# Seven products instead of eight in two groups of an expert layer, one bank copy more, and kept sums weighed in three steps

## The chip, the cores and the metric

The kernel runs on one core of one Trainium2 chip. The core has a matrix engine (TensorE, PE in the profile; PEld is its loading of weights), VectorE (DVE), ScalarE (ACT), GpSimd (POOL) and SyncE (SP, which here only issues transfers). The metric is the device time of one execution in microseconds; before the change the median of 4 runs is 928.86 us (928.18 to 929.29).

## The reference

A polynomial-sketch attention is followed by a mixture of eight experts whose weights come from eight rounds of Sinkhorn normalisation. All is fp32.

```python
# attention: B, H, S, D = 4, 4, 1088, 32; r = 8
phi(x) = outer product of (S1 x) and (S2 x), flattened      # 64 features
kv, z  = phi(k)^T v, sum over s of phi(k)
x      = (phi(q) kv) / (phi(q) z + 1e-6)    # laid out as N = 4352 rows of 128
# routing
P = exp(x @ w_gate - max)
8 times: P /= P.sum(1) + 1e-9;  P /= P.sum(0) + 1e-9;  P *= N / 8
# experts: F = 1024
out = sum over e of P[:, e] * (relu(x @ w1[e]) @ w2[e])
```

## The kernel before, in words

The experts are nearly all of the work, and the kernel starts them long before the routing weights exist. x is kept transposed (xT, 128 features by 4352 rows). The work is cut into **groups** (L647 to L656): a range of rows, cut into two or three tiles of n columns, and a list of experts.

- Groups 0 to 7 are **unweighted**: expert 0 on all 4352 rows, and expert 1 on rows 0 to 1280, computed without the routing weight, while attention and routing still run. Their results stay in SBUF as *kept sums* (kept[0], kept[1]) and are weighed later. Group 0 is rows 0 to 512 with n = 256 and expert 0, group 1 rows 512 to 1088 with n = 288 and expert 0, group 2 rows 0 to 512 with n = 256 and expert 1; groups 3 to 5 have n = 416, groups 6 and 7 n = 384.
- Groups 8 to 13 are **weighted**: x is multiplied by the expert's routing weight beforehand (POOL, L693, tile xe), so that the sums over the remaining experts add up in PSUM. Five of them have three tiles of 256 (twenty products for a block, from ten sums of pieces of w2, tile ws4, made by POOL at L242 for the first weighted group and stored in DRAM for the others), the last has two.

A group and an expert make an item, and an item is cut into blocks. A block has **steps**; each step is a first-layer product (x by w1, L929, two halves of 64 output columns side by side) with its relu by ScalarE (L933, tile hb or hx), and, eight steps late (LAG), the second-layer products of an earlier block (L1114, function into). These are half-width products too, two of which run beside each other. They add up in PSUM banks s0 to s3, and part(g, k) is called when bank k of a group has its last product.

For two tiles, the second layer is done in one of two ways:

- **eight** (L1017): the plain way, eight products for a block, no other work. part copies the two banks to kept (ScalarE, L736). Used by groups in DIRECT.
- **seven**: a Strassen-Winograd scheme (L1026). VectorE makes three subtractions for a block, one of double width (function less, L946, called at steps 4 and 5 after the block begins), the weights need four sums of w2 (tile ws, made by POOL at L203 to L206 in sums_of_two), and the seven sums of products, p1 to p7, lie in four banks. part_of_seven then recombines them: ScalarE copies halves of banks to tiles z, m, w, f and r (L762 to L777), and VectorE adds (L756 for those that are to go soon, in the next step, L753 for those at leisure). P1 lies in the lower half of bank 0, and L769 adds it, from the bank, to the copy m of bank 1.

What sets the order: DVE and PE run in the order of the program until some way into the last unweighted group, and the scheduler orders the other engines, except that instructions under keep_in_program_order keep theirs (POOL's weighings and their transfers among them). steps() is a generator that yields each step's share of time (n/480, and 16/15 of that for a group in DIRECT); fill(n) runs steps until n units are used up. The attention of batches 1 to 3 (function attention) and the routing (function routing) yield how many units of expert work are to go between their own pieces.

In attention(b), keys_sums is PE's L352 (it needs the key products, kp, L336), times(b, c) is VectorE's L468 and needs the tile rb from a transfer, keys_kept copies a key sum to kvs (VectorE L368), tops is PE's L477 with the bank from L472, over is VectorE's reading of that bank (L490 to L496), and keys_ab(b + 1) is PE's L319. The query transfers to qa and qb are issued in part by POOL.

weigh_kept (L709) weighs the kept sums of a weighted group's rows on POOL, each with a transfer of weights from pT to the tile pb, and adds them; steps() calls it in one of the group's experts. last_part writes the last group's two halves, y1 and y2.

Of the kernel before, what the change touches and what calls it, by code (L numbers as in the profile page):

```python
# [50 lines left out]
def kernel(  # L51
# [12 lines left out]
    nc = tc.nc  # L64
# [50 lines left out]
    own = consts.tile([P, H], F32, name="own")  # L115
# [36 lines left out]
    for i in range(2):  # L152
        t = wk.tile([P, H + 1, NT + 1, D], F32, name=f"v{i}", bufs=1)
# [487 lines left out]
    lower, upper = slice(0, H2), slice(H2, P)  # L641
# [8 lines left out]
    PLAIN = len(groups)  # L650


    DIRECT = (0, 1, 2)
    for lo in (1280, 512, 2048, 2816, 3584):
        groups.append((lo, NT3, 3, list(range(2 if lo == 512 else 1, E)), True))
    groups.append((0, 256, 2, list(range(2, E)), True))  # L656
# [2 lines left out]
    kept = [keep.tile([P, N], F32, name="kept0"), keep.tile([P, 1280], F32, name="kept1")]  # L659
# [4 lines left out]
    def direct_of(j):  # L664
        return items[j][0] in DIRECT

# [20 lines left out]
    def weights_of(e, lo, n, tag):  # L687
        pb = pools[0].tile([P, 3 * NT3], F32, tag=tag, name=tag)[:, 0:n]
        tc.keep_in_program_order(nc.sync.dma_start(out=pb, in_=pT[e:e + 1, lo:lo + n].to_broadcast([P, n])))
        return pb  # L690

    def weigh(out, x, pb):
        tc.keep_in_program_order(nc.gpsimd.tensor_tensor(out, x, pb, op=Alu.mult))  # L693
# [12 lines left out]

    first_weighted = next(j for j, (g, e) in enumerate(items) if g == PLAIN)

    def weigh_kept(g):  # L709

        lo, n, t, es, _ = groups[g]
        ys = []
        for e in range(es[0]):
            ys.append(kept[e][:, lo:lo + n * t])
            weigh(ys[e], ys[e], weights_of(e, lo, n * t, "pb"))
        for y in ys[1:]:
            tc.keep_in_program_order(nc.gpsimd.tensor_tensor(ys[0], ys[0], y, op=Alu.add))
        if t == 2:
            k1, k2 = ys[0][upper, 0:n], ys[0][upper, n:2 * n]
            tc.keep_in_program_order(nc.gpsimd.tensor_tensor(k1, k1, k2, op=Alu.subtract))  # L720
# [5 lines left out]
    def put(y, lo, n, queues):  # L726
        b0, nb = lo // 32, n // 32
        yt = pools[0].tile([P, NT3 // 32, 32], F32, tag="yt", name="yt", bufs=4)[:, 0:nb, :]
        nc.vector.transpose(out=yt.rearrange("p b d -> p (b d)"), in_=y)
        store(yt, b0, b0 + nb, queues)  # L730

    def part(g, k):

        if g in DIRECT:
            lo, n, _, es, _ = groups[g]
# [8 lines left out]
    def room(tag, n=NMAX):  # L744
        return keep.tile([P, NMAX], F32, tag=tag, name=tag)[:, 0:n]

    def part_of_seven(g, k):

        lo, n, _, es, _ = groups[g]
        s = sums[g][k]  # L750

        def add(out, a, b):
            at_leisure(lambda: nc.vector.tensor_tensor(out, a, b, op=Alu.add))  # L753

        def add_now(out, a, b):
            soon.append(lambda: nc.vector.tensor_tensor(out, a, b, op=Alu.add))  # L756

        own = parts.setdefault(g, {})
        y1, y2 = (kept[es[0]][:, lo + t * n:lo + (t + 1) * n] for t in range(2))
        if k == 0:  # L760
            z = own["z"] = room("z", n)
            nc.scalar.copy(z[lower], s[upper])  # L762
            nc.scalar.copy(z[upper], s[lower])
            add_now(z, s, z)
            own["p1"] = s
        elif k == 1:
            m = own["m"] = room("m", n)
            nc.scalar.copy(m, s)
            add_now(y1[lower], own["p1"][lower], m[lower])  # L769
        elif k == 2:  # L770
            w, f = own["w"], own["f"] = room("w", n), room("f", n)
            nc.scalar.copy(w[lower], s[lower])
            nc.scalar.copy(f[lower], s[upper])
            nc.scalar.copy(f[upper], s[upper])
        else:
            r = room("r", n)
            nc.scalar.copy(r[upper], s[lower])  # L777
            own["r"] = r
            own["p7"] = s
        own[k] = True  # L780
        z, w, f, m = (own.get(x) for x in "zwfm")
        if all(own.get(x) for x in (0, 2, 3)) and "v" not in own:
            own["v"] = True
            add_now(w[upper], own["p7"][upper], own["r"][upper])
            add(z, z, w)
            add(y2, z, f)
        if all(own.get(x) for x in range(4)):
            add(y1[upper], z[upper], m[upper])
# [9 lines left out]
    def last_part(g, k):  # L798


        lo, n, *_ = groups[g]
        s0, s1, s2, s3 = sums[g]

        def add(out, a, b):
            nc.vector.tensor_tensor(out, a, b, op=Alu.add)

        (y1, y2), z, w, x, f, r = last_rooms(g)
        if k == 3:
            nc.scalar.copy(r[upper], s3[lower])
            add(w[upper], s3[upper], r[upper])  # L810
        elif k == 0:
            nc.scalar.copy(z[upper], s0[lower])
            nc.scalar.copy(f, s0)
            add(x[upper], z[upper], w[upper])
            add(z[upper], x[upper], s0[upper])
        elif k == 2:
            nc.scalar.copy(r[lower], s2[upper])
            nc.scalar.copy(x[lower], s0[lower])
            add(y2[upper], z[upper], s2[upper])
            add(y2[lower], s2[lower], r[lower])  # L820
            put(y2, lo + n, n, (nc.sync, nc.scalar))
            add(x[upper], x[upper], s2[upper])
        else:
            add(y1, s1, x)
            put(y1, lo, n, (nc.sync, nc.scalar))
# [298 lines left out]
    def steps():  # L1124

        todo, sums_at, t = {}, {}, 0
        for k in range(len(blocks) + 5):
            if k == len(blocks) - 2:
                ctx.enter_context(tc.manual_schedule(engines={engines.DVE, engines.PE, engines.Activation}))
            if k == len(blocks):  # L1130
                for i, ps in enumerate(last_products()):
                    todo.setdefault(t + i, []).extend(ps)
            if k < len(blocks):
                j, q = blocks[k]
                g, e = items[j]
                lo, n, tiles, es, weighted = groups[g]
                if q == 0:
                    for i in (j, j + 1, j + 2 if 0 < j and j + 2 < first_weighted else j):
                        if i < len(items) and i not in sources and (pools or i < first_weighted):
                            prepare_x(i)  # L1140
                        if i < len(items) and i not in loaded_w and (pools or i < first_weighted):
                            prepare_w(i)
                if j == 0 and q == 2:
                    prepare_w(2)
                if q == 1 and j + 1 < first_weighted and not direct_of(j + 1) and loaded_w[j + 1][2] is None:
                    w1, w2, _ = loaded_w[j + 1]
                    w = w1, w2, sums_of_two(items[j + 1][1], w2)
                    loaded_w.update({i: w for i in loaded_w if items[i][1] == items[j + 1][1]})
                if q == 0:
                    if weighted and e == es[3 if tiles == 3 else 2]:  # L1150
                        weigh_kept(g)
                if k == len(blocks) - HELD:
                    kept_to_sums(g)
                m, step, sums_ = (four if tiles == 3 else two)(k)
                products = twenty if tiles == 3 else eight if g in DIRECT else seven
            for c in range(m if k < len(blocks) else 4):
                if k < len(blocks):
                    step(c)
                for do in sums_at.pop(t, ()):
                    do()  # L1160
                while soon:
                    soon.pop(0)()
                for b, p in todo.pop(t, ()):
                    second(b, p)
                if k < len(blocks) and c == 0:
                    for i in range(2, 10):
                        sums_at.setdefault(t + i, []).append(lambda i=i, f=sums_: f(i))
                    if k < len(blocks) - 2:
                        for i, ps in enumerate(products(k)):
                            todo.setdefault(t + LAG + i, []).extend((k, p) for p in ps)  # L1170
                share = n / 480 * (16 / 15 if g in DIRECT else 1)
                if k >= len(blocks):
                    while later:
                        later.pop(0)()
                elif later and (tiles == 3 or c % 2 or share > 0.9):
                    later.pop(0)()
                yield share
                t += 1
        while soon:
            soon.pop(0)()  # L1180
        while later:
            later.pop(0)()
# [105 lines left out]
```

## Time and profile before

| what | us |
|---|---|
| median of 4 runs | 928.86 |
| the profiled execution | 929.29 |
| its span in the trace | 927.5 |
| PE busy in the span | 913.6 |
| DVE, ACT, POOL busy | 675.8, 411.9, 210.9 |
| unweighted group 0: first product L929 | 16.9 |
| bank copies of group 2 (L736) end | 93.2 |
| routing's transfer to pT issued | 174.57 |
| first weighted product (L929 on xe) | 191.66 |
| last matmul ends | 920.8 |

Times on the trace count from the start of the span; the execution's own time is 1.8 us more than the span. An engine's row gives the start, the length, the engine, the line, the operation and its tiles (output<-inputs, partitions x elements), how many instructions are merged (x), and in brackets how long the engine had been idle before it and what released it. A matmul of fp32 is two instructions of PE, so the x of such a row counts twice.

### The profile page before, as it was taken

The page shows a single profiled execution, that of the slowest core. Times are in us where ns is not written, and L with a number is a line of the kernel's source. Part 1 is how long each engine was busy: PE and PEld are TensorE (multiplying, and loading weights), DVE is VectorE, ACT ScalarE, POOL GpSimd, SP SyncE. Part 2 cuts the span into 40 slices and gives each one's busy share as a digit, 9 for nine tenths or more (in the row PEclk, how much of TensorE's full clock was granted, in tenths as well). Part 3 has the DMA queues.
Part 4 walks back from the last instruction along what each step waited for, and adds up shares of the span by engine and source line. Part 5 has one row for each costly group of instructions (what it writes and reads, how often), then busy time and mean ns, then how long its engine had stood idle before and what let it go on. Part 6 is the DMA issues. An engine that isn't in the chain of part 4 may idle for free.

```text
span 927.5 us, 18876 instructions
## 1 busy us (share of the span) xinstructions
PE 913.6 (98%) x7466; PEld 544.9 (59%) x7466; DVE 675.8 (73%) x1140; ACT 411.9 (44%) x888; POOL 210.9 (23%) x220
## 2 busy tenths in 40 slices
PE   9999999999999999999999999999999999999997
PEld 6777444456666666655555555555555555556865
DVE  8544688797779797785976566966667977768665
ACT  3333455553444454434544444544445444446443
POOL 4021300093546402030120101101110234221120
PEclk9999999999999999999999999999999999999999
DMA  9994100213454445453445433363434366443640
GB/s 260 303 275 151 52 1 1 84 49 109 133 157 160 153 136 139 139 180 109 148 126 161 141 127 130 114 188 125 149 108 163 100 193 206 159 170 92 179 147 12
DMA packets 91303, 128.13 MB, mean 138 GB/s; under 512 B 25392, under 2 KB 69504, under 8 KB 86480
## 3 DMA queue, kind: packets, MB, share of 16 engines
q1 hardware_dynamic: 88384, 121.42, 42.1%
q0 software_dynamic: 1600, 5.36, 1.9%
q8 instruction: 58, 0.95, 0.4%
q10 hardware_dynamic: 1232, 0.16, 0.1%
q14 instruction: 29, 0.24, 0.1%
HBM read 107.88 MB, written 19.05 MB: 137 GB/s over the span
## 4 chain that ended last, share of the span: by engine, by line
PE 94%; DVE 4%; issue 1%; ACT 1%; DMA 0%; DVEq 0%; ACTq 0%
PE a L929 49%; PE s L1114 41%; PE a L352 1%; PE a L477 1%; DVE hb L993 1%; DVE hx L946 0%; PE a L319 0%; DVE pqg L993 0%; PE s L384 0%; PE a L441 0%; DMA raw<-in_S_dram 0%; ACT hb L933 0%; PE s L407 0%; DVE kept L756 0%; PE a L511 0%
## 5 line engine op out<-in xcount | busy, mean ns | idle before, releaser
L929 PE MATMUL a<-xe,w 128*64 128x256 f32 (+1 forms) x2560 | 517.3, 470 | 0.0
L933 ACT ACTIVATE hb<-a 128x256 f32<-128x256 f32 (+4 forms) x408 | 195.0, 479 | 258.5 <-PE a L929 230.6
L933 ACT ACTIVATE hx<-a 128x256 f32<-128x256 f32 (+1 forms) x360 | 167.2, 465 | 215.1 <-PE a L929 195.3
L929 PEld LDWEIGHTS a<-xe,w 128*64 128x64 f32 x2560 | 206.1, 137 | 80.6 <-issue 1.4
L1114 PE MATMUL s<-hb,ws 128*64 128x256 f32 (+2 forms) x1248 | 214.2, 395 | 0.6 <-DVE hb L993 0.6
L993 DVE TENSOR_TENSOR hx<-hx 128x512 f32<-128x512 f32 (+1 forms) x204 | 158.3, 785 | 65.3 <-ACT hx L933 59.9
L1114 PE MATMUL s<-hx,ws 128*64 128x256 f32 x1280 | 204.8, 379 | 0.7 <-DVE kept L756 0.7
L993 DVE TENSOR_TENSOR hb<-hb 128x512 f32<-128x512 f32 (+1 forms) x204 | 135.5, 675 | 92.9 <-ACT hb L933 88.8
L693 POOL TENSOR_TENSOR xe<-xT,xe 128x768 f32<-128x768 f32 (+2 forms) x41 | 81.3, 1983 | 497.9 <-DMA xe<-pT 450.3
L1114 PEld LDWEIGHTS s<-hx,ws 128*64 128x64 f32 x1280 | 105.9, 137 | 99.9 <-issue 73.4
L1114 PEld LDWEIGHTS s<-hb,ws 128*64 128x64 f32 x1248 | 102.0, 137 | 103.2 <-issue 79.9
L1114 PE MATMUL s<-hb,w 128*64 128x256 f32 (+3 forms) x616 | 116.4, 406 | 2.7 <-DVE kept L756 2.7
L929 PE MATMUL a<-xT,w 128*64 128x416 f32 (+3 forms) x512 | 117.3, 462 | 0.1
L1114 PEld LDWEIGHTS s<-hb,w 128*64 128x64 f32 x616 | 53.8, 137 | 36.0 <-issue 15.2
L1114 PE MATMUL s<-hx,w 128*64 128x256 f32 x384 | 68.3, 379 | 0.4 <-DVE hx L946 0.4
L242 POOL TENSOR_TENSOR ws<-w 128x256 f32<-128x256 f32 (+1 forms) x70 | 60.4, 897 | 15.7 <-PE a L929 13.1
L929 PEld LDWEIGHTS a<-xT,w 128*64 128x64 f32 x512 | 47.1, 137 | 28.3 <-issue 21.5
L946 DVE TENSOR_TENSOR hb<-hb 128x416 f32<-128x416 f32 (+3 forms) x60 | 46.3, 773 | 18.8 <-ACT hb L933 10.5
L946 DVE TENSOR_TENSOR hx<-hx 128x256 f32<-128x256 f32 (+1 forms) x65 | 39.5, 613 | 24.5 <-ACT hx L933 23.4
L993 DVE TENSOR_TENSOR pqg<-hb 128x512 f32<-128x512 f32 x68 | 45.1, 704 | 0.0
L1114 PEld LDWEIGHTS s<-hx,w 128*64 128x64 f32 x384 | 33.9, 137 | 11.4 <-DVE hx L946 0.8
L993 DVE TENSOR_TENSOR pqg<-hx 128x512 f32<-128x512 f32 x68 | 35.8, 566 | 0.0
(183 smaller groups left out, 467.5 us busy)
## 6 DMA issues: line engine op xcount, KB each, us to landing
w<-in_moe_w_dram SPq DMA_DIRECT2D x82, 512.0 KB, 5.5
ws<-ws SPq DMA_DIRECT2D x34, 1024.0 KB, 4.9
xe<-pT SPq DMA_DIRECT2D x34, 384.0 KB, 4.2
ws<-ws SPq DMA_DIRECT2D x12, 512.0 KB, 4.3
ph<-qa SPq DMA_DIRECT2D x12, 288.0 KB, 5.1
rb<-qb SPq DMA_DIRECT2D x3, 1152.0 KB, 8.2
pb<-pT SPq DMA_DIRECT2D x6, 384.0 KB, 7.5
kx<-in_k_dram SPq DMA_DIRECT2D x4, 544.0 KB, 4.2
```

Of the source, the lines that this page charges most:

```text
L242: tc.keep_in_program_order(nc.gpsimd.tensor_tensor(ws[:, c:c + len(ns)], blocks(x), blocks(y), op=Alu.subtract if off else Alu.add))
L352: nc.tensor.matmul(pv[64 * s:64 * (s + 1), i], kp[0:n, H * t + h].rearrange("p i j -> p (i j)"), vx[0:n, slots[h], t, :], start=(t == 0 an ...
L477: nc.tensor.matmul(pn[64 * s:64 * (s + 1), t, 2 * i:2 * i + 2].rearrange("p h d -> p (h d)"), ph[:, i, s, 64 * t:64 * (t + 1)], kvs[b % 2] ...
L693: tc.keep_in_program_order(nc.gpsimd.tensor_tensor(out, x, pb, op=Alu.mult))
L929: nc.tensor.matmul(ph[sl], loaded_w[j][0][:, P * f + H2 * s:P * f + H2 * (s + 1)], sources[j][:, lo:hi], start=True, stop=True, tile_posit ...
L933: nc.scalar.activation(out=out, in_=ph, func=Act.Relu)
L946: nc.vector.tensor_tensor(out, a, b, op=Alu.subtract)
L993: nc.vector.tensor_tensor(out if not isinstance(out, tuple) else places(*out), places(*a), places(*b) if isinstance(b, tuple) else b, op=A ...
L1114: nc.tensor.matmul(sums[g][i][H2 * s:H2 * (s + 1), n * place:n * (place + 1)], w, x, start=c == 1, stop=c == per, tile_position=(0, H2 * s))
```

## The change

Four edits:

- DIRECT shrinks from groups 0, 1 and 2 to group 0. Groups 1 and 2 are computed by seven, with all that belongs to it: VectorE's subtractions, part_of_seven for their banks, four PSUM banks in place of two, and their share in fill() without the factor 16/15. By the rule in steps(), POOL's four sums of w2 for expert 0 are then issued with the second block of group 0 (before: of group 2), and those for expert 1 with the second block of group 1 (before: of group 6).
- In part_of_seven, P1 is copied by ScalarE from the lower half of bank 0 to a tile named x, and L769's addition reads that tile instead of the bank.
- weigh_kept(g, i) does one piece of its work per call, and is called for the group's second, third and (where two experts were kept) fourth expert: first the weighing of kept[0], then that of kept[1], then the addition. Before, all came in one call, at the fourth expert of a three-tile group and the third of the last group.
- In last_part, the addition to x goes ahead of y2's transpose and its stores.

```diff
-    DIRECT = (0, 1, 2)
+    DIRECT = (0,)
...
-    def weigh_kept(g):
+    def weigh_kept(g, i):
 
         lo, n, t, es, _ = groups[g]
-        ys = []
-        for e in range(es[0]):
-            ys.append(kept[e][:, lo:lo + n * t])
-            weigh(ys[e], ys[e], weights_of(e, lo, n * t, "pb"))
+        ys = [kept[e][:, lo:lo + n * t] for e in range(es[0])]
+        if i < len(ys):
+            weigh(ys[i], ys[i], weights_of(i, lo, n * t, "pb"))
+            return
         for y in ys[1:]:
...
             nc.scalar.copy(z[lower], s[upper])
             nc.scalar.copy(z[upper], s[lower])
+            own["p1"] = room("x", n)
+            nc.scalar.copy(own["p1"][lower], s[lower])
             add_now(z, s, z)
-            own["p1"] = s
...
             add(y2[lower], s2[lower], r[lower])
+            add(x[upper], x[upper], s2[upper])
             put(y2, lo + n, n, (nc.sync, nc.scalar))
-            add(x[upper], x[upper], s2[upper])
...
-                    if weighted and e == es[3 if tiles == 3 else 2]:
-                        weigh_kept(g)
+                    if weighted and 1 <= es.index(e) <= es[0] + 1:
+                        weigh_kept(g, es.index(e) - 1)
```

## The prediction

> **What bounds the kernel now.** I read the page's busy shares first, then PE's list of waits, then the timelines of single engines around each wait. The busy shares say who could be the bound:
>
> ```profile
> PE 913.6 (98%) x7466; PEld 544.9 (59%) x7466; DVE 675.8 (73%) x1140; ACT 411.9 (44%) x888; POOL 210.9 (23%) x220
> PE 94%; DVE 4%; issue 1%; ACT 1%; DMA 0%; DVEq 0%; ACTq 0%
> ```
>
> PE is busy for 98% of the span, at a granted clock of 1.00 in every stage asked for, and 94% of the chain that ended last is PE. So time falls by the matmuls that go and by the waits PE is spared, and rises by new waits of PE. All its waits that this change can touch are in three rows (in all, times, longest):
>
> ```profile
> PE s L1114 <- DVE kept L756: 3.4, 4, 1.2
> ...
> PE s L1114 <- DVE hb L993: 0.6, 1, 0.6
> PE s L1114 <- DVE hx L946: 0.4, 1, 0.4
> ```
>
> The first row is the group boundary: the next group's first product into bank 0 waits until VectorE has added P1, read from that bank, to P2 (L769). Here it is on the timeline; VectorE came late because the routing chain stood before it:
>
> ```profile
> 118.17 0.57 DVE L756 TENSOR_TENSOR kept<-s,m 64x416 f32<-64x416 f32 x1
> 118.80 0.56 PE L1114 MATMUL s<-hb,w 128*64 128x416 f32 x1 [1.19 <-DVE kept L756]
> ```
>
> The second row is a VectorE that crawls while POOL weighs the kept sums in one burst. The same pair of subtractions (pqg), ten microseconds earlier and then beside POOL:
>
> ```profile
> 390.69 1.02 DVE L993 TENSOR_TENSOR pqg<-hx 128x512 f32<-128x512 f32 x2
> 400.14 4.03 POOL L693 TENSOR_TENSOR kept<-kept,pb 128x768 f32<-128x768 f32 x2 [12.37 <-DMA pb<-pT]
> 400.16 4.29 DVE L993 TENSOR_TENSOR pqg<-hb 128x512 f32<-128x512 f32 x2
> 408.96 0.65 PE L1114 MATMUL s<-hb,ws 128*64 128x256 f32 x4 [0.59 <-DVE hb L993]
> ```
>
> **The change part by part.** The profiled execution took 929.29 us, 1.8 more than its span of 927.5; the median of the four runs is 928.86. I sum against 929.29 and take the same difference off the median.
>
> *Fewer products.* Groups 1 (n=288) and 2 (n=256) have four blocks each; each block loses one of eight half-width products. Two halves run side by side, so one product is worth half the spacing of such pairs. Two neighbouring rows give the spacings, 0.43 us for 256 columns and 0.48 (0.485 between other rows) for 288:
>
> ```profile
> 66.37 0.60 PE L929 MATMUL a<-xT,w 128*64 128x256 f32 x4
> 66.80 0.66 PE L1114 MATMUL s<-hb,w 128*64 128x288 f32 x4
> 67.28 0.60 PE L929 MATMUL a<-xT,w 128*64 128x256 f32 x4
> ```
>
> 4 x 0.215 + 4 x 0.2425 = 1.83 us off, if the lone seventh product is really half a pair. It is: in group 7 (384 columns, pair 0.645) one block of four first-layer pairs and 3.5 second-layer pairs takes 182.63 to 187.47 = 4.84 us, and 7.5 x 0.645 = 4.84.
>
> *What the seven products need.* Each block now has one double-width subtraction and two single ones on VectorE (L946). From rows of 768, 512, 416 and 256 columns (0.96, 0.69, 0.61, 0.43 us) I take 0.76 + 2 x 0.46 = 1.68 us for 288 and 0.69 + 2 x 0.43 = 1.55 for 256; four of each, and six recombining additions of about 0.45 per group: 12.9 + 5.4 = 18.3 us more VectorE. It lands between 40 and 100 us, where VectorE is busy 6.6, 12.0 and 11.0 of each 20 us: room in total. But VectorE is in order, and stands still in front of a transfer:
>
> ```profile
> 59.95 0.96 DVE L468 TENSOR_TENSOR ph<-ph,rb 128x768 f32<-128x768 f32 x1 [7.43 <-DMA rb<-qb]
> 60.94 0.23 DVE L368 COPY kvs<-a 64x66 f32<-64x66 f32 x1
> 61.93 0.92 PE L477 MATMUL a<-kvs,ph 128*64 128x66 f32 x24
> ```
>
> Counting units in steps() against fill(), the subtractions of group 1's last block are issued between the first and second row. The copy then ends at 59.95 + 0.96 + 1.68 + 0.23 = 62.8; PE, with one more step ahead of L477, gets there at 62.2 and starts at 62.9 at best: 0.7 us of wait. From there to 78.8 VectorE had 11.3 us of work; about 7.3 is added (four blocks less the last one or so, and group 1's additions), 18.6 in 16.2 us. It falls behind: walking the program order with these durations, the key products of batch 3 (L336) end at 83.4 where PE wants them at 82.5 (before: done at 78.7 for 82.1): 1.0 us more. The boundaries into groups 2 and 3 I put at 0.2. Against that, the 0.48 us that PE lost ahead of L477 at 87.50 goes, since PE has one step more to do there. Sum +1.4; bounds -0.5 (all covered) and +3.5 (1.6 more if L477 of the second third finds the bank of the first, L472, still read until about 68.0 when PE is there at 66.4, and 0.5 for a longer backlog). ScalarE copies eight banks or halves per group instead of two, 0.37 to 0.40 us each, and is busy 7.7 of 20 us there: nothing.
>
> POOL's sums of w2 (2.9 us from 64.35, 4.3 from 98.99) are issued some 40 us sooner, behind the query DMAs that end at 17.5 and 41.1; they are wanted at 49 and 71. Nothing; without that cover, up to 3 us.
>
> *P1 copied.* Bank 0 is then free after the addition of z instead. It ended at 114.81, 140.51, 162.44, 181 and 200.12 us; PE wanted the bank at 117.61, 140.36, 162.15, no wait, and 202.42 (start less wait). With 0.06 of signalling, 0.2 + 0.35 of the 3.4 us stays: 2.85 off. The copy (64 partitions, 0.48 to 0.50 us by L763's rows) stands behind the two z copies, which end 0.03 to 2.9 us before VectorE's addition; even if that waits 0.5 longer, it is in time at the first and last boundary and hidden by VectorE's queue at the middle two. What is late next is that addition: before the second boundary it stood behind a routing step that ended at 138.89 and two subtractions, and started at 139.93. Bounds: 1.0 off (a shorter wait takes its place at each) to 3.4 (the boundaries move by 1.24 of 95.6 units against the routing yields, which puts z ahead of the chain at both middle ones).
>
> A rule speaks against this. The Trainium skill, SBUF — State Buffer, section "Who interferes with whom", states that a VectorE operation with two SBUF inputs and a GpSimd operation that reads SBUF block each other for a whole instruction, while one SBUF input does not contend. P1 from a bank was one SBUF input; now there are two. The crawl at 400 us agrees. By the rule an addition beside POOL would take perhaps 1 us longer; as PE no longer waits for it, the sum stays.
>
> *Weighing spread.* The burst (two weighings and an addition, then the next x, 8.2 us on POOL) put VectorE 6.1 us late (4.29, 2.30, 3.10 for 1.02, 0.69, 1.48). Cut into parts of about 4 us each beside one x, it is some 3 us late, under the 5.5 us that it had to spare (6.1 less PE's wait of 0.59). The last group's burst (878.95 to 885.86) likewise. 0.59 + 0.35 = 0.94 off; I take 0.8, bounds 0.94 off and 0.5 on: in the first weighted group the weighing moves into experts whose sums POOL makes itself, but there 278.64 to 292.28 was one unbroken burst and PE did not wait. The pb transfers go one by one, and no queue is held.
>
> *The end.* The x addition (0.42) goes ahead of y2's transpose. VectorE does both before y1 either way, and y2's stores have 1.5 us before y1's: 0, within 0.1.
>
> *The start of the weighted part.* PE comes 1.83 us sooner after the routing than before. x was weighed at 187.4 for a use at 191.66, and its transfer stood behind w2, freed by PE at 180.2, which moves along: covered.
>
> Sum: -1.83 + 1.4 - 2.85 - 0.8 = -4.1: 925.2 for such an execution, 924.8 as a median.
>
> **The rivals.** (1) *Everything is covered*: the walk is too strict (transfers land earlier, PE is already behind). -1.83 - 0.3 - 3.2 - 0.9 = -6.2: 922.6. That VectorE is idle for 30 of the 60 us from 40 to 100 speaks for it, and that it sheds 1.2 us at 99 (three L946 rows took 3.44 beside POOL's sums, 2.28 without); that it was idle in in-order waits speaks against. (2) *The waits change places*: 2.9 in the attention, 1.0 off at the boundaries, 0.5 off for the weighing: -0.4, 928.4. The late z at two boundaries speaks for it. (3) *VectorE becomes the bound from 60 to 90 us*: held by rb, each attention step of batches 2 and 3 makes PE wait in turn: 0.7 and 1.8 at L477, 0.5 at L319, 2.0 at the key products, 0.9 at L477 of batch 3, and 1.2 (the longest boundary before) at each of the two new boundaries: 8.3. -1.83 + 8.3 - 2.85 - 0.8 = +2.8: 931.7. It decides from 7.4 us lost there. For it: 18.6 us of work in 16.2. Against: VectorE was free from 79.7 to 86.1, and PE asks for most results four steps after they are issued. (4) The change doing less than it says: p7 unpaired gives back 1.8, which lands in case 2.
>
> **How the numbers follow.** A measurement tells 0.2% (1.9 us) from no change. My forecast 0.47 (923.6 to 926.9), rival 1 0.20, rivals 2 and 4 0.20, rival 3 0.13. So faster 0.67, same 0.20, slower 0.13. The range takes in rival 1 and most of rival 2: 922.0 to 929.6.
>
> **What would show it.** Matmul rows of PE 7466 - 16 = 7450; VectorE 1140 + 36; PE's wait for kept L756 gone, a wait for z of at most 0.6 left; the waits for hb L993 and hx L946 gone; new waits of PE at L477 near 62 us and at L352 near 82. Wrong if PE's idle time between 55 and 95 us grows by over 3.5 us, or if boundary waits stay above 1.5 in all.

## The result, and the profile after

The changed kernel takes 926.41 us (median of 43 runs, 924.60 to 929.04), the kernel before 929.16 (median of 63 runs beside them). The ratio is 0.9972, 95% interval 0.9967 to 0.9978: 2.6 us off (2.0 to 3.1). The forecast was 924.8. The profiled execution took 926.81, its span is 925.0. Lines behind L764 have moved by one: L929, L946, L993 and L1114 of before are L930, L947, L994 and L1115.

The page's busy shares, and the chain that ended last:

```profile
PE 913.4 (99%) x7450; PEld 615.0 (66%) x7450; DVE 688.7 (74%) x1176; ACT 417.8 (45%) x905; POOL 212.6 (23%) x220
...
PE 97%; DVE 1%; ACT 1%; issue 1%; POOL 0%; DVEq 0%; ACTq 0%; POOLq 0%
```

Sixteen matmul rows fewer and 36 VectorE instructions more, as counted ahead. But look at PE's busy time: 913.4 us, against 913.6 before. Sixteen rows went and the time that PE is busy stayed. That is the first sign that a step of the sum failed. (PE counts as busy while only a part of it works.) PE's waits (in all, times, longest):

```profile
PE a L477 <- issue: 2.5, 1, 2.5
...
PE a L477 <- ACT m L769: 1.0, 1, 1.0
...
PE s L1115 <- DVE w L756: 0.3, 1, 0.3
```

The longest is the one at the first L477, 2.5 us (1.3 before); it is taken up under "The start". The 3.4 us for kept, 0.6 for hb and 0.4 for hx are gone; 0.3 is left at one boundary. Neither wait that the forecast put into the attention is in this profile's list (L477 near 62 us, L352 near 82); the first turns up in a later one. A wait at L477 of batch 3 has grown from 0.5 to 1.0. VectorE's timeline at the boundary that was shown of before:

```profile
116.60 0.59 DVE L756 TENSOR_TENSOR z<-s,z 128x416 f32<-128x416 f32 x1 [0.60 <-ACT x L765]
117.41 0.58 DVE L756 TENSOR_TENSOR kept<-x,m 64x416 f32<-64x416 f32 x1 [0.21 <-ACT m L769]
118.08 0.29 DVE L602 TENSOR_REDUCE mx<-a 128x1 f32<-128x128 f32 x1
```

The addition to kept stands here ahead of the routing chain (L602 onward), where it stood behind it before. So it would be early even if it still read the bank. That is two reasons for one wait to go, and the experiments have to separate them. The kept sums' weighing, on VectorE and on POOL:

```profile
398.88 1.02 DVE L994 TENSOR_TENSOR pqg<-hb 128x512 f32<-128x512 f32 x2
```

```profile
378.82 1.82 POOL L693 TENSOR_TENSOR kept<-kept,pb 128x768 f32<-128x768 f32 x1 [10.47 <-DMA pb<-pT]
...
387.16 2.00 POOL L717 TENSOR_TENSOR kept<-kept,kept 128x768 f32<-128x768 f32 x1
```

The pair for pqg takes 1.02 us now; before, it took 4.29 beside the burst.

To compare kernels I cut each span at four instructions that all of them have: the first L477, the first product on xe (first weighted), the first product s<-hx, and the first of the last additions on VectorE (w, L805, or L806 after). In us:

| | to first L477 | to first xe | to first s<-hx | to last w | to the end | span |
|---|---|---|---|---|---|---|
| before | 34.25 | 157.40 | 11.45 | 716.15 | 8.25 | 927.5 |
| changed | 35.72 | 154.93 | 10.53 | 714.95 | 8.91 | 925.0 |
| difference | +1.47 | -2.47 | -0.92 | -1.20 | +0.66 | -2.5 |

The second and third stretch hold all four boundaries and all products that went: 3.39 off. The fourth is the weighted part, and the last is the end, which the forecast had at 0.

### The profile page after: what moved, and what is told of

It is laid out like the page before. It is cut to its first block, busy times and chain, and to the rows that moved or that the text cites. A ratio compares the mean times of both kernels' runs of the same rounds, so it can differ in the third digit from the quotient of the medians.

```text
span 925.0 us, 18903 instructions
## 1 busy us (share of the span) xinstructions
PE 913.4 (99%) x7450; PEld 615.0 (66%) x7450; DVE 688.7 (74%) x1176; ACT 417.8 (45%) x905; POOL 212.6 (23%) x220
## 4 chain that ended last, share of the span: by engine, by line
PE 97%; DVE 1%; ACT 1%; issue 1%; POOL 0%; DVEq 0%; ACTq 0%; POOLq 0%
PE a L930 51%; PE s L1115 42%; PE a L352 1%; PE a L477 1%; PE a L114 1%; PE a L319 0%; PE a L441 0%; PE s L384 0%; PE a L511 0%; PE s L407 0%; DVE kp L336 0%; PE a L390 0%; PE a L407 0%; ACT hb L934 0%; DVE qT L302 0%
## 5 line engine op out<-in xcount | busy, mean ns | idle before, releaser
L930 PE MATMUL a<-xe,w 128*64 128x256 f32 (+1 forms) x2560 | 561.2, 470 | 0.0
L930 PEld LDWEIGHTS a<-xe,w 128*64 128x64 f32 x2560 | 246.9, 137 | 65.3 <-issue 1.1
L1115 PE MATMUL s<-hb,ws 128*64 128x256 f32 (+3 forms) x1312 | 252.7, 395 | 0.3 <-DVE w L756 0.3
L1115 PE MATMUL s<-hx,ws 128*64 128x256 f32 x1280 | 230.0, 379 | 0.0
L994 DVE TENSOR_TENSOR hb<-hb 128x512 f32<-128x512 f32 (+1 forms) x204 | 136.9, 681 | 98.1 <-ACT hb L934 94.0
L994 DVE TENSOR_TENSOR hx<-hx 128x512 f32<-128x512 f32 (+1 forms) x204 | 151.2, 751 | 62.0 <-ACT hx L934 56.8
L1115 PEld LDWEIGHTS s<-hb,ws 128*64 128x64 f32 x1312 | 128.1, 137 | 87.3 <-issue 60.8
L1115 PEld LDWEIGHTS s<-hx,ws 128*64 128x64 f32 x1280 | 125.1, 137 | 78.8 <-issue 53.8
L930 PE MATMUL a<-xT,w 128*64 128x416 f32 (+3 forms) x512 | 120.7, 463 | 0.1
L1115 PE MATMUL s<-hb,w 128*64 128x256 f32 (+3 forms) x536 | 113.3, 408 | 0.0
L1115 PE MATMUL s<-hx,w 128*64 128x256 f32 x384 | 74.7, 379 | 0.0
L947 DVE TENSOR_TENSOR hb<-hb 128x416 f32<-128x416 f32 (+7 forms) x84 | 58.0, 692 | 15.4 <-ACT hb L934 11.5
L930 PEld LDWEIGHTS a<-xT,w 128*64 128x64 f32 x512 | 51.2, 137 | 24.7 <-issue 10.9
L1115 PEld LDWEIGHTS s<-hb,w 128*64 128x64 f32 x536 | 53.5, 137 | 20.9 <-issue 6.3
L242 POOL TENSOR_TENSOR ws<-w 128x256 f32<-128x256 f32 (+1 forms) x70 | 62.2, 922 | 7.2 <-DMA w<-in_moe_w_dram 7.2
L947 DVE TENSOR_TENSOR hx<-hx 128x256 f32<-128x256 f32 (+1 forms) x65 | 38.6, 597 | 24.2 <-ACT hx L934 23.1
L1115 PEld LDWEIGHTS s<-hx,w 128*64 128x64 f32 x384 | 38.8, 137 | 8.1
L994 DVE TENSOR_TENSOR pqg<-hb 128x512 f32<-128x512 f32 x68 | 43.2, 676 | 0.0
L994 DVE TENSOR_TENSOR pqg<-hx 128x512 f32<-128x512 f32 x68 | 36.1, 570 | 0.0
```

The lines of the kernel that those rows point to most:

```text
L242: tc.keep_in_program_order(nc.gpsimd.tensor_tensor(ws[:, c:c + len(ns)], blocks(x), blocks(y), op=Alu.subtract if off else Alu.add))
L930: nc.tensor.matmul(ph[sl], loaded_w[j][0][:, P * f + H2 * s:P * f + H2 * (s + 1)], sources[j][:, lo:hi], start=True, stop=True, tile_posit ...
L947: nc.vector.tensor_tensor(out, a, b, op=Alu.subtract)
L994: nc.vector.tensor_tensor(out if not isinstance(out, tuple) else places(*out), places(*a), places(*b) if isinstance(b, tuple) else b, op=A ...
L1115: nc.tensor.matmul(sums[g][i][H2 * s:H2 * (s + 1), n * place:n * (place + 1)], w, x, start=c == 1, stop=c == per, tile_position=(0, H2 * s))
```

## Experiments

**Each part alone.** The first three are the kernel before with one edit each.

```diff
+            own["p1"] = room("x", n)
+            nc.scalar.copy(own["p1"][lower], s[lower])
             add_now(z, s, z)
-            own["p1"] = s
```

> The kernel before with one edit: P1 is copied out of its bank by ScalarE; no other part of the change. Forecast's step: all that the boundaries gave comes from the copy: 2.85 us off, 926.3, the row of PE's wait for kept gone and at most 0.6 us of waits for z in its place. Rival: it is the place of the boundaries against the routing chain, which only the fewer products move: then the addition of z stands behind the chain at the two middle boundaries, and the copy alone gives 1.0 to 1.8 off, 927.4 to 928.2, with 1.5 us or more of waits for z.

Measured: 925.07, ratio 0.9963 (0.9947 to 0.9979). The forecast's step holds, and a little more: from the first L477 to the first s<-hx 168.85 us are 165.50. VectorE's order is that of before; the kept addition is still late, but PE no longer waits for it:

```profile
114.87 0.59 DVE L756 TENSOR_TENSOR z<-s,z 128x416 f32<-128x416 f32 x1 [0.60 <-ACT x L765]
...
118.16 0.66 DVE L617 TENSOR_REDUCE cs<-p 128x8 f32<-128x280 f32 x1
118.74 0.58 DVE L756 TENSOR_TENSOR kept<-x,m 64x416 f32<-64x416 f32 x1
```

and its waits have in place of the 3.4 us only:

```profile
PE s L1115 <- DVE z L756: 0.5, 2, 0.4
```

Next, the seven products alone:

```diff
-    DIRECT = (0, 1, 2)
+    DIRECT = (0,)
```

> The kernel before with one edit: seven products for eight in groups 1 and 2; P1 still read from its bank, the weighing still in one burst. Forecast's steps: 1.83 off, 1.4 on in the attention, boundaries as before: 928.7, with about 3 us of PE's wait for kept left. Rival (the shifted boundaries are what removed that wait): 1.83 off, 1.4 on, 2.5 to 3.4 off: 925.3 to 926.2, and under 0.9 us of waits for kept.

Measured: 925.38, ratio 0.9957 (0.9939 to 0.9975). The rival wins. P1 is still read from its bank, yet no wait for kept is left, since the boundaries have moved against the routing's yields, and the addition now comes first:

```profile
114.44 0.58 DVE L756 TENSOR_TENSOR kept<-s,m 64x416 f32<-64x416 f32 x1 [0.34 <-ACT m L768]
115.49 0.29 DVE L602 TENSOR_REDUCE mx<-a 128x1 f32<-128x128 f32 x1 [0.46 <-PE s L1114]
```

The last of the three is the edit to weigh_kept and its call, alone:

> The kernel before with one edit: the kept sums are weighed over three experts. Forecast's step: 0.8 off (0.94 if both rows go): 928.4, the waits for hb and hx at the ends of the two bursts gone. Rival: VectorE was late there but the wait comes back at another step: no change, 929.2.

Measured: 928.00, ratio 0.9988 (0.9977 to 0.9998): 1.1 off (0.2 to 2.1). Both waits are gone. The weighted stretch of its profile falls by 1.84, from 716.15 to 714.31. Between the kernel with the copy alone and that with copy and spread weighing (below), the weighted stretch falls from 715.32 to 714.30; between the two with seven products from 715.75 to 715.02.

So copy alone gave 3.7 off by the medians (3.4 by the ratio), seven products alone 3.4 (4.0), spread alone 0.8 (1.1): together some 8, and the whole change gave 2.6.

**The start.** In the profile of the changed kernel the first L477 is 1.47 us late, because VectorE's first multiplication waits for the transfer rb (L461):

```profile
34.40 0.96 DVE L468 TENSOR_TENSOR ph<-ph,rb 128x768 f32<-128x768 f32 x1 [6.23 <-DMA rb<-qb]
```

POOL's sums of w2 for expert 0 now stand right behind its query transfers, so I moved them:

```diff
-                if q == 1 and j + 1 < first_weighted and ...
+                if q == (1 if j else 3) and j + 1 < first_weighted and ...
```

> The changed kernel with one edit: POOL's four sums of expert 0's second weights are made in the fourth block of group 0 and not in its second, some 20 us later and so not right behind POOL's query transfers. If the sums beside those transfers made rb land late (first L468 at 34.4 us against 32.9 in the kernel before, of which 0.4 was there at 15 us already): about 1 us off, 925.3, and PE's wait at L477 near 35 us back to some 1.3. If that lateness is the scatter of one execution: no change, 926.4, and in the repeated profile the first L468 falls anywhere from 32.9 to 34.4.

Measured: 925.62, ratio 0.9961 (0.9947 to 0.9976). This tells little: the time is 0.8 lower, the intervals overlap, L468 starts at 33.25, and PE waits at two places, 0.9 us ahead of the first L477 and 1.3 us at L319, of which the second is not in the list of the changed kernel. The same changed kernel once more, beside variants:

> The changed kernel as it is, beside its own variants. From the profiles: from the first L477 to the first product of the weighted part 3.4 us less than before, behind it 0.98 less (the spread weighing), and from the last w addition to the end 0.62 more: 3.8 off, if the 1.5 us that it came later to the first L477 was the scatter of one execution; 2.7 off, as first measured, if that lateness belongs to the kernel.

Measured: 926.66, ratio 0.9967 (0.9954 to 0.9980). Here L468 starts early, with the very same program:

```profile
32.53 0.96 DVE L468 TENSOR_TENSOR ph<-ph,rb 128x768 f32<-128x768 f32 x1 [4.53 <-DMA rb<-qb]
```

So the lateness at the start is the scatter of that transfer: over the 14 profiles of this study the first L477 starts between 32.91 and 35.72. But this execution lost 1.7 us in the second stretch (156.62 for 154.93), for the most part where the forecast had looked: L477 of batch 2 started at 64.15 after 1.36 us of waiting. VectorE's rows ahead of it:

```profile
61.17 0.96 DVE L468 TENSOR_TENSOR ph<-ph,rb 128x768 f32<-128x768 f32 x1 [4.61 <-DMA rb<-qb]
62.05 1.74 DVE L947 TENSOR_TENSOR hb<-hb 128x576 f32<-128x576 f32 x3
63.81 0.23 DVE L368 COPY kvs<-a 64x66 f32<-64x66 f32 x1
```

The subtractions of group 1's last block stand between the multiplication that waits for rb and the copy that L477 wants, as the forecast's walk had it (1.68 us there, 1.74 here). With eight products the copy follows L468 at once: 59.95 and 60.94 before. In the profile shown first, rb came before PE needed it (L468 at 59.46, L477 at 64.19, no wait named there), since PE itself was late from the first L477. A late rb thus cost this kernel 1.36 us here. Does the kernel before have that in hand? At one lateness the profiles allow the comparison: L468 starts 26.4 us behind the first L477 in the kernel with the late sums and 26.5 behind it in the one with the spread weighing alone, and L477 of batch 2 then waits 0.76 with seven products and 0.06 with eight. No profile with eight products has rb as late as here (27.3 us), so that part is not shown. Among the ten profiles with seven products L477 of batch 2 waits in three: 0.76 with the late sums, 1.36 here, 2.32 in the last but one run below; in the four with eight products it waits 0.06 at most. By the medians the change is 2.5 off here, and 2.75 in the first comparison.

**The end.** The changed kernel with the order of before in last_part:

```diff
-            add(x[upper], x[upper], s2[upper])
             put(y2, lo + n, n, (nc.sync, nc.scalar))
+            add(x[upper], x[upper], s2[upper])
```

> The changed kernel with the end as it was before: y2 is transposed and stored ahead of the last addition to x. Forecast's step (0, within 0.1): no difference. Rival: the later y2 crowds its stores and y1's on the two queues, and that costs 0.62: the end, from the last w addition (first of the nine on VectorE) to the end of the span, is 8.2 us and not 8.85, and the time is 0.6 less than that of the changed kernel.

Measured: 924.99, ratio 0.9960 (0.9946 to 0.9974); the medians on one chip differ by 1.7, with overlapping intervals. The last stretch took 8.66 here. In all ten other profiles with the old order (before's among them) it took 8.20 to 8.30, in the three with the new order 8.84, 8.91 and 8.95. So the new order costs 0.6, and one execution of the old one came within 0.2 of it. The stores of out in the kernel before:

```profile
DMA to landing us min/median/max: 1.6/1.8/1.9
```

and in the changed kernel:

```profile
DMA to landing us min/median/max: 1.7/2.1/2.4
```

Measured from the w addition (919.26 before, 916.13 after), y2's first store is issued at 3.3 us before and 3.8 after; the last one starts at 5.2 and 5.6. The addition takes 0.42 on VectorE ahead of y2's transpose, y1's transpose ends no sooner (4.76 and 4.70), and the eight stores now go out in one crowd and take up to 2.4 us to land.

**Without the copy, and without the seven products.** Both have the old end and the spread weighing.

> As the variant with the old end, and without the copy of P1: seven products and spread weighing alone. Forecast's step: without the copy the boundaries take their 2.85 back: 2.85 slower than with it, and 3 us of waits for kept. Rival (the boundaries that the fewer products shift are free of the wait by themselves): within 0.4 of the variant with the copy, rather faster, since the copy delays z ahead of the copy kvs (wait at L477 of batch 3: 0.6 without, 1.0 with it).

Measured: 924.76, ratio 0.9955 (0.9942 to 0.9967). The copy is worth nothing beside the seven products; 154.76 us from first L477 to first xe, 154.90 with it. What it costs is seen in the changed kernel at batch 3, on ScalarE and then on VectorE:

```profile
88.58 0.36 ACT L765 COPY x<-s 64x256 f32<-64x256 f32 x1
```

```profile
88.97 0.42 DVE L756 TENSOR_TENSOR z<-s,z 128x256 f32<-128x256 f32 x1 [1.37 <-ACT x L765]
89.43 0.23 DVE L368 COPY kvs<-a 64x66 f32<-64x66 f32 x1
```

This is the third copy out of the bank, behind the two for z, of which the addition of z needs nothing; but it starts 0.03 us behind its end, as at 116.60 above. VectorE's copy of kvs, which L477 wants, is queued behind it: PE waits 1.0 there with the copy and 0.6 without. The Trainium skill's page "PSUM — Partial Sum Buffer", section "PSUM bank collisions raise a hardware error", says that the compiler's scheduler makes any two instructions of different engines wait for each other when they touch the same bank and quadrant, two reads included. Both rows here agree with that.

> As the variant with the old end, but eight products in groups 1 and 2 as before: the copy and the spread weighing alone. The seven products are worth -1.83 + 1.4 = -0.4 where the copy already frees the boundaries: 0.4 slower than with them, some 4.2 off the time before. Rival: what VectorE loses in the attention is less (covered): 1.8 slower than with them. Other rival: it is more, and this one is the faster.

Measured: 924.90, ratio 0.9958 (0.9946 to 0.9970): as fast as with the seven products. 154.96 us from first L477 to first xe, with 16 matmul rows more. The forecast's difference of 0.4 cannot be told from none here. Up to the first xe the seven products are 0.1 to 0.2 ahead by the stretches, but the weighted stretch is longer with them (714.93 with the copy and 715.02 without, against 714.30). Part of that is only where the cuts fall: one product of group 7 stands behind the first xe with seven products and ahead of it with eight. The whole way from the first L477 to the last w, which is free of this, takes 879.8 us with eight products and 880.3 to 880.4 with seven. So by these three profiles the seven are 0.5 to 0.6 behind, less than the times can tell.

**Where the 1.83 us of the products went.** Between the kernels with and without them PE's listed waits hardly differ. So I looked at single rows. Where rows of the same length follow, a lone product does find a partner: in the kernel with seven products (copy, old end) rows of two different products stand beside each other from 54.03 on, two rows every 0.24 us. That ends when a stage of the attention with 64-column rows comes in:

```profile
56.94 0.33 PE L352 MATMUL a<-v,kp 128*64 128x64 f32 x2
57.18 0.41 PE L1115 MATMUL s<-hb,ws 128*64 128x288 f32 x1
57.42 2.40 PE L352 MATMUL a<-v,kp 128*64 128x64 f32 x70
```

The row at 57.18 runs alone, and the stage goes on behind it: the half pair is lost. The seventh product of group 1's last block stands behind that stage, with the first layer of the next block behind it:

```profile
60.29 0.65 PE L1115 MATMUL s<-hb,ws 128*64 128x288 f32 x2
61.03 0.65 PE L930 MATMUL a<-xT,w 128*64 128x256 f32 x4
```

With eight products there are four rows at the same place, at 60.73, and the next step at 61.47. Two rows take 0.74 us there, just as four do. But a lack of a partner does not explain all of that: behind the 0.485 us of the rows neither half works for 0.25, in both kernels, until ScalarE has ended the relu of the step before:

```profile
60.57 0.41 ACT L934 ACTIVATE hb<-a 128x288 f32<-128x288 f32 x1 [0.49 <-PE a L930]
```

It ends at 60.98, and PE goes on at 61.03; with eight products it ends at 61.42, and PE goes on at 61.47. Here ScalarE sets the step, and a product more or less changes nothing.

From the start times of all matmul rows I added up, between first L477 and first xe, the time in which only one half was at work and that in which none was, each row counted with 0.8415 ns per column (0.2425 us for 288):

| kernel (all with spread weighing and old end, but for the first) | one half | none | stretch |
|---|---|---|---|
| before | 4.06 | 7.01 | 157.40 |
| copy, eight products | 4.18 | 4.51 | 154.96 |
| seven products, no copy | 8.45 | 3.99 | 154.76 |
| seven products, each seventh twice | 7.36 | 5.04 | 157.16 |
| seven products, pairs in groups 1 to 3 | 5.93 | 5.46 | 155.05 |
| seven products, stages as before | 6.02 | 7.97 | 157.52 |

(In the three rows whose stages have moved, some 0.8 us of the first column is a single quarter of PE at work in L511; more on this below.) Four microseconds more with one half idle are two microseconds of PE: what the products saved. Three kernels test this. First, a twin for each lone product:

```diff
+        twin = [(ws[:, 2, q], ts[1], 3, 1 - k % 2, 0)] if items[j][0] in (1, 2) else []
...
-            return bank0, [p2, p4], bank2, [p7]
-        return bank0[::-1], [p4, p2], bank2[::-1], [p7]
+            return bank0, [p2, p4], bank2, [p7, *twin]
+        return bank0[::-1], [p4, p2], bank2[::-1], [p7, *twin]
```

(The number of products that the bank's sum counts is raised to match.)

> Seven products and spread weighing (no copy of P1, the end as before), and in groups 1 and 2 the seventh product is issued on both halves of PE, so that P7 is counted twice there: eight products' worth of rows with seven products' operands. Theory (a lone seventh product finds no partner between the attention's stages and takes a whole pair's time): no dearer than one, 924.8, and from the first L477 to the first weighted product 154.8 us as without the twin. Rival, the forecast's step (a lone one is half a pair): 1.83 slower, 926.6, and 156.6 us.

Measured: 925.47, ratio 0.9963 (0.9950 to 0.9975). The stretch is 157.16, but 1.53 of it lies ahead of the first 288-column product of the second layer, where the program is the same and PE's granted clock fell to 0.50 for a while (16.51 us for 14.98; more on this at the end); 155.6 is left, and in the table 6.2 and 4.1. So sixteen rows more cost 0.9 us, half of what the forecast's step wants and more than the theory's nothing: both miss. Of the 0.9, 0.4 is no cost of the rows: L511 takes 3.13 us in this profile and 2.76 without the twin (below). So the lone products had saved 0.5 to 0.9 of the 1.83. At the place shown above the twin was indeed free: four rows from 62.02, the next step at 62.76, 0.05 behind the relu's end.

Second, pairs made on purpose:

```diff
                         for i, ps in enumerate(products(k)):
+                            if i == 3 and k % 2 and g in (1, 2, 3):
+                                i = -1
                             todo.setdefault(t + LAG + i, []).extend((k, p) for p in ps)
```

> Seven products and spread weighing (no copy of P1, the end as before), and in groups 1 to 3 the seventh product of each odd block is issued five steps sooner, right behind that of the even block, on the other half. Theory (the lone products run alone): two now make one pair, 1.83 off for groups 1 and 2 and up to 0.3 more for group 3, 922.7 to 923.0; from the first L477 to the first weighted product 152.6 to 153.0 us and not 154.8. Rival (the time that the seven products did not give is lost in VectorE's work): no change, 924.8, or slower by waits for t13, which must now be ready a step sooner.

(By the edit it is four steps, from index 3 to -1.) Measured: 924.31, ratio 0.9953 (0.9940 to 0.9966), and the stretch 155.05: not the gain expected. The table shows why: time on one half falls by 2.5 us (1.26 of PE), and time with no half at work rises by 1.47. There are waits that were not there, 0.4 us at L511 (shown below) and these among them:

```profile
PE a L929 <- ACT hb L933: 0.6, 1, 0.6
...
PE s L1114 <- DVE hb L946: 0.3, 1, 0.3
```

> As the variant that pairs the seventh products of groups 1 to 3, but in all seven groups with seven products ahead of the weighted part. Where no attention stage stands between two blocks they find each other already, so no more than 0.3 off that variant, 922.5 to 922.9. Rival: the routing chain on VectorE makes t13 late, and PE waits for it up to 1 us.

Measured: 926.37, ratio 0.9975 (0.9965 to 0.9986): slower than pairing three groups, by 2 us. L477 of batch 2 waited 2.32 us in this profile (L468 at 60.86), and behind the first product of group 3, where the routing runs, the time on one half rose from 2.4 to 3.8 us. Of the waits named by the rival there is 0.3 us for a subtraction (hb L946), the same as with three groups; which part of the rest is scatter is open.

Third, the stages put back to their old steps, without the copy:

```diff
-                share = n / 480 * (16 / 15 if g in DIRECT else 1)
+                share = n / 480 * (16 / 15 if g < 3 else 1)
```

> Seven products and spread weighing (no copy of P1, the end as before), and each step of groups 1 and 2 is counted against the attention's and the routing's yields as in the kernel before (16/15 of its share), so that every stage and every boundary stands at the same step as there. Theory (the 1.24 units by which the boundaries move are what freed them): PE's wait for kept is back, 2.7 to 3.4 us; and if the move of the stages is also what cost PE pairs between the first product of group 3 and the first block of group 6 (56.9 us there with seven products, 55.9 with eight, no wait in it), that stretch is 0.9 to 1.0 shorter beside those waits: 926.4 to 927.2 in all. Rival (something else in the seven products freed the boundaries): 924.8, no wait for kept over 0.3.

Measured: 928.01, ratio 0.9988 (0.9977 to 0.9999). The wait for kept is back in full:

```profile
PE s L1114 <- DVE kept L756: 3.4, 4, 1.2
```

and so is its cause, the addition behind the chain:

```profile
115.69 0.29 DVE L602 TENSOR_REDUCE mx<-a 128x1 f32<-128x128 f32 x1
...
119.05 0.57 DVE L756 TENSOR_TENSOR kept<-s,m 64x416 f32<-64x416 f32 x1
```

That settles the boundaries: the move of 1.24 units frees them by itself, and so does the copy. The median is 0.8 above the expected range; the profile has a wait at L441 for VectorE's qT that is longer than elsewhere (1.1 us, 0.3 before). The one-half time is down to 6.0, 1.84 above that of eight products: 0.92 us, lost with the stages in place, nearly all of it in rows that end alone ahead of a stage or a relu, as shown above. This is near the 0.9 to 1.3 that the twin leaves.

The other 2.4 us of one-half time (some 1.2 us) came with the move. Half of it lies behind group 3's first product of the second layer, up to the first block of group 6, where the same matmuls run: 2.59 with the stages moved, 1.36 with them in place, 0.92 with eight products. Without the time in which no half works, the stretch is 0.5 us shorter with the stages in place than with them moved (55.4, 55.9), and not the expected 0.9 to 1.0. The whole stretch takes 56.9 us with the stages moved and 55.9 with eight products. 0.7 of this 1.0 stands in one place, L511, the routing's product: four quarter-width products side by side, one for each batch. First with eight products, then with seven and no copy:

```profile
106.11 2.04 PE L511 MATMUL a<-xT,wg 128*32 128x512 f32 x24
```

```profile
106.09 2.76 PE L511 MATMUL a<-xT,wg 128*32 128x512 f32 x24
```

In the second, one of the four starts 0.75 us behind the other three, at 106.85, and ends alone. It starts 0.13 us after the last transfer to xT has landed (106.72). In all nine profiles whose stages have moved, that transfer lands 0.5 to 1.3 us after the first of the four has started, the last of the four starts 0.13 to 0.14 us behind the landing, and L511 takes 2.64 to 3.41 us. In the five with the stages in place, with eight products or with seven, it has landed 0.3 to 1.2 us ahead, and L511 takes 2.04. The kernel just measured, which differs from the one without the copy in the stages alone, is one of the five. As three quarters of PE are at work meanwhile, the list of waits does not show it, but for a part in the kernel with pairs in three groups:

```profile
106.58 1.99 PE L511 MATMUL a<-xT,wg 128*32 128x512 f32 x18 [0.37 <-DMA xT<-xd]
```

So of the 1.83, some 0.9 goes to lone products that end alone, and 0.7 to L511, which the moved stages bring ahead of its transfer. What is left is not taken apart.

## Why the prediction was right or wrong

The range held the time, as did the narrower one of the forecast's own case (923.6 to 926.9), and the direction and "faster" were right. The forecast was 1.6 us too low, and its terms were further off than its sum: that the sum came so near is in part luck.

- *Fewer products, -1.83*: **wrong**. The step that failed is that "the lone seventh product is really half a pair". That was measured in group 7, where long rows follow each other without a break, and carried to groups 1 and 2, where stages of the attention cut in and a step can wait for ScalarE anyway. Some 0.9 is lost that way, and 0.7 more at L511, which the forecast did not look at. Net, the term is -0.1 to -0.2 up to the first xe, and +0.5 to +0.6 up to the last w.
- *Seven products' needs, +1.4*: **half right**. The first place is right in mechanism and depends on when rb lands: 0 to 2.3 us at L477 near 62, 0.7 forecast. The second, the key products of batch 3, is in no profile's list of PE's waits. And where I had put a gain of 0.48, at L477 of batch 3, there is 0.5 more, most of it from the copy of P1.
- *P1 copied, -2.85*: **right** in mechanism, and somewhat small: 3.35 by the stretches of the kernel with the copy alone. But in this change the copy is not what gives it. The forecast had the other reason as the far end of its range ("the boundaries move by 1.24 of 95.6 units"); it is enough by itself, and the two do not add. The rule that the prediction set against the copy shows, but costs PE nothing: at the last boundary the addition with two inputs in SBUF took 1.08 us beside POOL's sums (L242) in the kernel with the copy alone; before, with P1 in its bank, 0.54 beside the same sums.
- *Weighing spread, -0.8*: **right**; -0.7, -1.0 and -1.8 by the weighted stretches of the three pairs of kernels with and without it, -1.1 (0.2 to 2.1) by the time of the kernel with it alone. Both waits went.
- *The end, 0*: **wrong**, +0.6. The step looked at what VectorE does ahead of y1 and counted the 1.5 us between y2's and y1's stores as room. Pushing y2's stores toward y1's makes the last one start 0.4 us later and take longer to land.
- *POOL's sums sooner, nothing*: not shown otherwise.
- *Rivals*: "everything is covered" holds only in executions in which rb is early, and was wrong on the products. VectorE as the bound did not come: PE's list has no wait for t13. The fourth, "p7 unpaired gives back 1.8", names the term that failed, and some 0.9 of it came; its time, 928.4, did not, since the boundaries and the weighing gave in full.

The sum came out near because the errors went both ways: the products gave some 1.7 less than forecast up to the first xe and the end 0.6, the boundaries and the weighing together some 0.9 more. The stretches of the first profile without the start give 2.47 + 0.92 + 1.20 - 0.66 = 3.9 off, and the measured time is 2.6 off. In both profiles of the changed kernel 1.5 to 1.7 us were lost, most of it to rb, once ahead of the first L477 and once at that of batch 2. The second belongs to the kernel (the subtractions behind L468); for the first, moving POOL's sums decided nothing. How much of the missing 1.3 us each makes stays open.

Five versions are as fast as each other, with ratios of 0.9953 to 0.9960: copy and spread without seven products; seven and spread without the copy; both; the pairs in three groups; and seven products alone. The simplest of them is the last, one line of the change, with 0.9957 (0.9939 to 0.9975). No run here tells the five apart, nor surely from the changed kernel: its two comparisons gave 0.9972 (0.9967 to 0.9978) and 0.9967 (0.9954 to 0.9980).

## What to carry to other kernels

When a change has several parts, ask of each wait how many of them would remove it: two cures of one wait count once, and a part that merely shifts the order can be one of them. Price a removed instruction by what its neighbours do with the room, at the place where it is removed; a half-width product saves time only if work for the other half can start at once. Where an array works in parts, look at single rows for a part that waits: the list of waits has only the times at which all of it stood still. At the end of a kernel, look at the stores too: here, holding back the first ones by 0.5 us made the last land 0.6 later.

## What the hardware showed

A pair of half-width fp32 products of 288 columns (four rows) took 0.48 us of PE (66.80 to 67.28 before), and the two rows of one such product without a partner followed each other at 0.24 (60.29 and 60.54 in the kernel with the copy and the old end): alone, it takes as long as the pair. The Trainium skill's page "TensorEngine Tiling (Array Packing)", section "Overview", gives "Up to 2×" where a dimension is at most 64 and independent tiles work side by side. Here that held for pairs in an unbroken stream, and about half of what the lone products should have saved was lost where another stage followed.

VectorE and ScalarE reading the same bank went one behind the other (0.03 us between the copy's end and the addition's start, twice), though neither wrote it; the profile names the copy as what released the addition.

The same program had its first L477 at 33.85 us in one execution and at 35.72 in another. The transfer that it waits for (rb, 1,152 KB) took 6.1 to 9.0 us to land over the 14 profiles.

Behind such a wait PE's clock fell once. In the kernel with the twins, PE stood still for 2.09 us ahead of the first L477, and the next stretches are these (the third figure from the end is the granted clock):

```profile
34.00:36.00 2.00, 1.12 (x32) 1.10 (x34) 1.94 (x4) 0.00 (x0) 0.00 (x0) 1.00 1.05 366
36.00:38.00 2.00, 2.00 (x12) 1.39 (x10) 1.97 (x3) 0.38 (x1) 0.00 (x0) 0.50 1.17 223
```

A step of four rows took 0.85 us there for 0.43, and from 38 to 40 us the mean clock was 0.65. In the changed kernel's profile PE stood still longer at the same place, 2.46 us, and the clock stayed at 1.00. The Trainium skill's page "TensorE: Matmul & The Clock Gate", section "What's actually happening" of its Part 1, has the clock fall after an idle window of about 3.4 us; here 2.09 us was enough once, and 2.46 was not. Of the executions of the changed kernel in the first comparison, the five with a mean granted clock of 0.997 or less have a median of 928.1 us, and the 25 with 0.999 or more one of 926.1: a part of the scatter, though not of the missing microsecond.
